# Two band-v transfers at the head of the sync queue joined into one, with the identity matrix behind it

## Chip, cores and metric

The kernel runs on one core of one Trainium2 chip. The metric is device microseconds (us) of one execution; the time before is 297.66 us, the median of three runs (297.59 to 299.77).

## What is computed

The reference is a sparse attention layer followed by a feed-forward block. q, k and v have the shape (8, 8, 576, 64): batch, heads, positions, head size. Heads 0 to 3 use a local band mask (a position sees itself and the 31 before it), heads 4 to 7 a strided causal mask (positions that are equal modulo 32).

```
scores = q @ k^T / 8, masked with -1e9       # per batch and head
attn   = softmax(scores)
x      = (attn @ v), heads side by side      # (4608, 512)
h      = x @ w_in                            # (512, 2048)
g      = s * relu(h)**2 + b
out    = g @ w_out                           # (2048, 512), float32
```

## The kernel before

The work is emitted by a planner (`Plan`, `lay_out`): every matmul group is a step with a cost and with needs, and a small model of the five engines decides in which order the steps of attention, of the first feed-forward product (`ff1`) and of the second (`ff2`) are written. The order is fixed when the kernel is built. On the chip each engine walks its own list in order and waits on semaphores.

A batch element has four pairs of heads: m = 0 and 1 are the band pairs (names with `_loc`, tiles of 96 queries, `LQ`), m = 2 and 3 the strided ones (`_str`, tiles of 72). For the first batch element q and k arrive with positions on partitions and are transposed on TensorE by a matmul against an identity matrix, the tile `ident` (L527 for the band pairs). The results go to PSUM and are copied by ScalarE or VectorE to `qD_loc` and `kT_loc` (L437). Then the scores of a tile are two matmuls into one bank: L653 adds the mask, as `ident` times `negs`, and L656 adds k times q. ScalarE takes the exponential (L674), L717 multiplies by v, VectorE normalises (L734, L744), and `x_nat` is transposed back (L764).

There are two ways for data to come in. GpSimd (POOL) issues the transfers that change fp32 to fp16, one after the other in its own list: `ql` and `kl` of the first pair, `ql` and `kl` of the second (L378), `qs` and `ks` (L405), v of the second band pair (L1399), `vs` (L405). SyncE (SP) issues plain copies. At its head stood, in this order: `ident` (L346, 128 rows of 256 bytes), v of head 0 and v of head 1 in the band layout (L344, each 96 partitions by 6 runs of 64 fp32 numbers, so 576 runs of 256 bytes), and `negs` (L348, 128 rows of 672 bytes). Behind them SP waits for `ql` of the second pair (L1396), and only then issues `masks` and the two scalars.

The two heads of v land as fp32 in `vl_stage`, which is a view of the later home of `w_out` (so the trace calls it `w_out_sb`), and POOL casts them to `v_loc` (L437, one cast for each head, then a copy of the 32 rows that lie before a tile). Only after that, and after a small copy that waits for `qs` (L1420), does POOL issue the four transfers of `w_in` (L427).

While PE waits in the first 14 us, the planner writes filler matmuls into its list (`keep_running`, L1536), which multiply a tile of ones into a bank that nobody reads. Their number and place are fixed when the kernel is built.

Of the kernel before, what the change touches and what calls it, by code (L numbers as in the profile page):

```python
# [204 lines left out]
@with_exitstack  # L205
def kernel(
    ctx: ExitStack,
    tc: tile.TileContext,
    q: bass.AP,
    k: bass.AP,  # L210
    v: bass.AP,
    moe_w_in: bass.AP,
    moe_w_out: bass.AP,
    moe_s: bass.AP,
    moe_b: bass.AP,
    out: bass.AP,
):
    shapes = q.shape, out.shape, moe_w_in.shape
    lay_out(ctx, tc, tc.nc, q, k, v, moe_w_in, moe_w_out, moe_s, moe_b, out, ORDER, *shapes)


def lay_out(ctx, tc, nc, q, k, v, moe_w_in, moe_w_out, moe_s, moe_b, out, order, q_shape, out_shape,
# [14 lines left out]
    LQ, LT, LPAD = 96, 6, 32  # L237
# [64 lines left out]
    def x_free(b):  # L302
# [23 lines left out]
    vl_stage = w_out_sb.rearrange("p f m -> p (f m)").bitcast(FP32)[:, 0:NL // 2].rearrange(  # L326
        "p (h t d) -> p h t d", h=2, d=D)
# [7 lines left out]
    def v_band(b, h):  # L335

        return v[b, h].rearrange("(t p) d -> p t d", p=LQ)
# [1 line left out]
    def h4(ap):  # L339
        return ap.rearrange("p (h x) -> p h x", h=4)  # L340

    def stage_v(heads):
        for h in heads:
            nc.sync.dma_start(out=vl_stage[LPAD:128, h], in_=v_band(0, h))  # L344

    nc.sync.dma_start(out=ident, in_=h_ident.ap())  # L346
    stage_v(range(2))
    nc.sync.dma_start(out=negs, in_=h_neg.ap())  # L348
    nc.vector.memset(ones16, 1.0)
    for i in range(2):  # L350
# [1001 lines left out]
    def fetch_qk(b):  # L1352
        for mm in range(2):
            if (b - 1, "kTs", mm) in loaded:

                nc.gpsimd.tensor_copy(out=gate[0:1, 2 + mm:3 + mm],  # L1356
                                      in_=loaded[b - 1, "kTs", mm][0:1, 0, 0:1])
        load_qk(b)
        for name in ("q", "k"):
            if b >= (QB_DMA if name == "q" else KB_DMA):  # L1360
                arrive(both(name + "l", b), landing(4600))
                continue
            if b < HEAD_T:
                arrive(both(name + "l", b), landing(2400 if name == "q" else 2600))
                continue
            plan.done["raw", name, b] = landing(1700 if b > 1 else 2400 if name == "q" else 2500)
            for mm in range(2):
                pair_post(b, name, mm, ("raw", name, b))
        for name in ("qs", "ks"):
            arrive(both(name, b), landing(2000 if b > 1 else 1200))  # L1370
# [23 lines left out]
    def after_landing(i, src):  # L1394
# [5 lines left out]
        out=v_loc[0].rearrange("p h t d -> p (h t) d")[LPAD:128, 2 * LT:4 * LT, 0:D],  # L1400
        in_=v.rearrange("b h (t p) d -> b p (h t) d", p=LQ)[0, :, 2 * LT:4 * LT])
# [58 lines left out]
    for b in range(B):  # L1460
        for m in range(4):
            steps, last_av = pair_steps(b, m)
            att.append(steps)
            if b + 2 < B:

                if m == 0:
# [5 lines left out]
                        lambda eng, b=b: fetch_qk(b + 2), [("fetch", b + 2)])  # L1472
# [157 lines left out]
```

## Time and profile before

| what | value |
|---|---|
| median of three runs | 297.66 us (297.59 to 299.77) |
| profiled execution, its own time | 298.37 us |
| span of the profiled execution | 296.5 us |
| PE busy | 289.6 us, 98% of the span |
| PEld, DVE, ACT, POOL busy | 74%, 80%, 66%, 31% |
| DMA, software queue (issued by POOL) | 60848 packets, 18.23 MB |
| DMA, hardware queue (issued by SP) | 45270 packets, 19.51 MB |
| granted TensorE clock, mean | 1.00 |

The span runs from the first to the last instruction that the profiler records; the time of the same execution is 1.9 us longer than its span. "Busy" is time in which an engine has an instruction running; a line such as L527 is a line of the kernel before; an arrow `out<-in` gives the tile written and the tiles read. Rows of DMA issues on SP carry the name SPq. In a view of one queue the columns are packets, megabytes, and the time of the packets as a share of sixteen DMA engines over the stretch asked for.

### The profile page before, as it was taken

How to read it: one execution, taken by the hardware profiler on the slowest of the kernel's cores; microseconds unless marked ns; L12 is line 12 of the kernel's file. 1: busy time of each engine (PE TensorE's matmuls, PEld its weight loads, DVE VectorE, ACT ScalarE, POOL GpSimd, SP SyncE). 2: the span in 40 equal slices, each digit the busy share in tenths (PEclk: the TensorE clock that was granted, in tenths of full speed). 3: DMA queues.
4: the chain of work that ended last, by engine and by line, in shares of the span. 5: the costliest groups of instructions: out<-in, count | busy, mean ns of one | idle time of the engine just before them, and what ended most of it. 6: DMA issues, size and time to landing. Idle time of an engine off the chain costs nothing.

```text
span 296.5 us, 7100 instructions
## 1 busy us (share of the span) xinstructions
PE 289.6 (98%) x2800; PEld 218.9 (74%) x2800; DVE 236.3 (80%) x498; ACT 194.4 (66%) x334; POOL 92.2 (31%) x140
## 2 busy tenths in 40 slices
PE   7999999999999999999999999999999999999995
PEld 3775665665565567889767885778888999999984
DVE  5865977888976789768886888688799689888873
ACT  3677855897967797948873777477966564576500
POOL 8772623700970395007920087200001000000000
PEclk9999999999999999999999999999999999999999
DMA  8999999999999899959999999998230300210314
GB/s 131 190 207 203 205 177 179 202 189 130 136 155 156 100 90 170 164 109 132 175 145 137 165 168 149 146 127 211 47 93 20 108 35 2 71 38 2 107 39 143
DMA packets 106152, 38.19 MB, mean 129 GB/s; under 512 B 85414, under 2 KB 103974, under 8 KB 106118
## 3 DMA queue, kind: packets, MB, share of 16 engines
q0 software_dynamic: 60848, 18.23, 65.4%
q1 hardware_dynamic: 45270, 19.51, 36.6%
q8 instruction: 22, 0.36, 0.6%
q14 instruction: 12, 0.10, 0.1%
HBM read 36.99 MB, written 10.62 MB: 161 GB/s over the span
## 4 chain that ended last, share of the span: by engine, by line
PE 78%; DMA 15%; POOL 4%; issue 1%; DVE 1%; ACT 0%; SPq 0%; POOLq 0%; DVEq 0%
PE ps_f L1016 28%; PE ps_f L984 22%; PE ps_f L1271 6%; DMA v_loc<-in_v_dram 5%; DMA ks<-in_k_dram 5%; PE ps_s L656 4%; PE ps_f L1241 3%; DMA kT<-ks 3%; DMA vs<-in_v_dram 2%; PE ps_a L717 2%; PE ps_t L1241 2%; PE ps_a L1241 2%; PE ps_s L1241 2%; PE ps_s L984 2%; PE ps_t L984 1%; PE ps_s L1271 1%
## 5 line engine op out<-in xcount | busy, mean ns | idle before, releaser
L1016 PE MATMUL ps_f<-xT,w_in_sb 128*128 128x512 f16 (+4 forms) x568 | 115.3, 331 | 0.0
L1042 ACT ACTIVATE u<-ps_f 128x512 f16<-128x512 f32 x107 | 62.8, 594 | 34.5 <-PE ps_f L1016 32.4
L1016 PEld LDWEIGHTS <-w_in_sb 128*128 128x128 f16 x576 | 57.1, 114 | 23.1
L984 PEld LDWEIGHTS <-gT 128*128 128x128 f16 x608 | 58.3, 98 | 8.6
L984 PE MATMUL ps_f<-w_out_sb,gT 128*128 128x256 f16 x376 | 53.4, 273 | 0.0
L1271 PE MATMUL ps_f<-w_out_sb,gT 128*128 128x512 f16 x112 | 31.9, 379 | 0.0
L674 ACT ACTIVATE p_str<-ps_s 72x432 f16<-72x432 f32 (+1 forms) x45 | 21.1, 487 | 10.4 <-PE ps_s L656 9.8
L1052 DVE TENSOR_TENSOR gT<-u 128x1024 f16<-128x1024 f16 x32 | 21.8, 682 | 5.2 <-ACT u L1042 4.8
L1050 ACT ACTIVATE gT<-u 128x1024 f16<-128x1024 f16 x24 | 25.4, 1058 | 0.7
L984 PE MATMUL ps_f<-w_mix,gT 128*128 128x256 f16 x176 | 24.9, 273 | 0.0
L674 ACT ACTIVATE p_loc<-ps_s 128x384 f16<-128x384 f32 x46 | 20.7, 489 | 5.9 <-PE ps_s L656 5.4
L744 DVE TENSOR_TENSOR x_nat<-ps_a,rec 72x384 f16<-72x384 f32 (+2 forms) x45 | 23.5, 523 | 0.7
L852 DVE TENSOR_TENSOR gT<-gT 128x1024 f16<-128x1024 f16 x34 | 22.4, 683 | 0.3 <-ACT gT L1050 0.3
L415 POOL DMA_DIRECT2D v_loc<-in_v_dram x24 | 17.8, 762 | 9.6 <-DVE x_nat L744 3.7
L984 PEld LDWEIGHTS <-S 128*128 128x128 f16 x176 | 17.1, 98 | 2.8
L717 PEld LDWEIGHTS <-p_str 72*128 72x128 f16 x256 | 13.6, 98 | 5.7 <-ACT p_str L674 0.7
L1271 PEld LDWEIGHTS <-gT 128*128 128x128 f16 x128 | 11.4, 98 | 6.9 <-issue 0.2
L420 POOL DMA_DIRECT2D v_str<-in_v_dram x16 | 13.0, 816 | 11.0 <-PE ps_f L1016 3.5
L1356 POOL COPY gate<-kT 1x1 f16<-1x1 f16 x6 | 1.6, 266 | 47.1 <-DMA kT<-ks 47.1
L734 DVE RECIPROCAL rec<-ps_a 72x6 f32<-72x6 f32 (+2 forms) x45 | 8.3, 184 | 9.0 <-PE ps_a L717 8.8
L717 PEld LDWEIGHTS <-p_loc 128*128 128x128 f16 x192 | 11.2, 98 | 5.3 <-ACT kTs L437 0.8
L984 PE MATMUL ps_f<-w_mix,S 128*128 128x256 f16 x112 | 15.0, 273 | 0.0
(233 smaller groups left out, 542.2 us busy)
## 6 DMA issues: line engine op xcount, KB each, us to landing
out_dram<-o SPq DMA_DIRECT2D x34, 256.0 KB
w_in_sb<-in_moe_w_in_dram POOLq DMA_DIRECT2D x4, 512.0 KB, 10.4
w_out_sb<-in_moe_w_out_dram POOLq DMA_DIRECT2D x4, 512.0 KB, 9.8
qs<-in_q_dram POOLq DMA_DIRECT2D x6, 288.0 KB, 7.6
ks<-in_k_dram POOLq DMA_DIRECT2D x6, 288.0 KB, 9.4
v_loc<-in_v_dram POOLq DMA_DIRECT2D x24, 72.0 KB, 10.5
ql<-in_q_dram POOLq DMA_DIRECT2D x4, 288.0 KB, 9.7
kl<-in_k_dram POOLq DMA_DIRECT2D x16, 72.0 KB, 4.1
```

The source lines that it names most:

```text
L415: nc.gpsimd.dma_start(out=vl[LPAD:128, h, :, 0:D], in_=v_band(b, h))
L674: nc.scalar.activation(out=st["pw", g][0:nk, 0:2 * n * nq], in_=st["s", g][0:nk, 0:2 * n * nq], func=AF.Exp, scale=scale)
L717: nc.tensor.matmul(out=st["pa", g][:, n % 6, :], lhsT=st["pw", gp_][0:nk, i * nq:i * nq + WIDE], rhs=vt[0:nk, 2 * mm + e, j, :])
L744: nc.vector.tensor_tensor(out=x_at(0, cnt), in0=st["pa", g][0:nq, 0:cnt, 0:D], in1=st["rec", g][0:nq, 0:cnt].to_broadcast([nq, cnt, D]), o ...
L852: {"V": nc.vector, "P": nc.gpsimd}[eng].tensor_tensor(out=at(out), in0=at(x), in1=at(y), op=op)
L984: nc.tensor.matmul(out=gts[name, T, t][:, 0] if halves else gts[name, T][:, t], lhsT=lhs(k, t), rhs=rhs(k), start=fresh and k == 0 and (ha ...
L1016: nc.tensor.matmul(out=gts["h", T, ft][:, lo:hi], lhsT=w_in_sb[ft // 4][:, ct].rearrange("p (x l) -> p l x", l=4)[:, ft % 4], rhs=xT[ct][: ...
L1042: nc.scalar.activation(out=u, in_=gts["h", T, ft], func=AF.Relu)
L1050: nc.scalar.activation(out=g, in_=u, func=AF.Square)
L1052: nc.vector.tensor_tensor(out=g, in0=u, in1=u, op=ALU.mult)
L1241: nc.tensor.matmul(out=st[bk][:, 256 * t:256 * t + 256], lhsT=lhs(t, c), rhs=rhs(c), start=fresh and t == c == 0, stop=t == c == 1, skip_g ...
L1271: nc.tensor.matmul(out=gts[id_], lhsT=gts[T][:, ft, ts * 128:(ts + 1) * 128], rhs=w_out_sb[:, ft, cols], start=(ft == 0), stop=(ft == NFT ...
```

## The change

The helper `stage_v` and its call are removed. In its place one transfer brings both heads of v: partition p takes 12 runs of 64 numbers (2 heads by 6 tiles) instead of 6 in each of two transfers. It stands first in the list of SP, `ident` second, `negs` third. Source, destination, and the bytes of every run are the same.

```diff
-    def stage_v(heads):
-        for h in heads:
-            nc.sync.dma_start(out=vl_stage[LPAD:128, h], in_=v_band(0, h))
-
+    nc.sync.dma_start(
+        out=vl_stage[LPAD:128].rearrange("p h t d -> p (h t) d"),
+        in_=v.rearrange("b h (t p) d -> b p (h t) d", p=LQ)[0, :, 0:2 * LT])
     nc.sync.dma_start(out=ident, in_=h_ident.ap())
-    stage_v(range(2))
     nc.sync.dma_start(out=negs, in_=h_neg.ap())
```

The lists of PE, DVE, ACT and POOL keep their instructions and their order; SP's has one transfer fewer. The first transpose of PE (L527) waits for `ident` as before, now the second transfer of SP; both casts of POOL now depend on the one transfer of v, where each depended on its own. The lines of the changed kernel are numbered two lower from there on.

## The prediction

> **What bounds the kernel now.** I read the page first (busy shares), then who waited for whom on PE, then the rows of the first 10 us in order of time, then the DMA queues over short stretches of those microseconds.
>
> ```profile
> PE 289.6 (98%) x2800; PEld 218.9 (74%) x2800; DVE 236.3 (80%) x498; ACT 194.4 (66%) x334; POOL 92.2 (31%) x140
> ```
>
> PE is busy for 289.6 of 296.5 us, and the stretches 60 to 120, 120 to 180 and 240 to 290 us show it busy all the time. So a microsecond lost at the start moves the end by a microsecond, unless an early wait of PE takes it up. The waits of PE, longest first:
>
> ```profile
> PE ps_t L527 <- DMA ql<-in_q_dram: 1.1, 1, 1.1
> PE ps_s L1536 <- DVE w_mix L349: 1.1, 1, 1.1
> PE ps_f L717 <- DVE v_loc L437: 0.7, 1, 0.7
> ```
>
> The first is the place of the change: the first transpose needs `ql` and `ident`, and `ql` came last. The rows around it (start, duration, engine; behind x the count, in brackets the idle time before):
>
> ```profile
> 0.74 0.35 SPq L346 DMA_DIRECT2D ident<-ident  x1
> 1.16 0.99 SPq L344 DMA_DIRECT2D w_out_sb<-in_v_dram  x2
> 2.19 0.52 SPq L348 DMA_DIRECT2D w_mix<-negs  x1
> ...
> 1.06 3.68 PE L1536 MATMUL ps_s<-w_mix 128*128 128x512 f16 x10 [1.06 <-DVE w_mix L349]
> 5.84 0.45 PE L527 MATMUL ps_t<-ident,ql 96*64 96x96 f16 x12 [1.10 <-DMA ql<-in_q_dram]
> 6.22 0.94 PE L1536 MATMUL ps_s<-w_mix 128*128 128x256 f16 x6
> 7.09 0.45 PE L527 MATMUL ps_a<-ident,kl 96*64 96x96 f16 x12
> 7.46 0.77 PE L1536 MATMUL ps_s<-w_mix 128*128 128x512 f16 x3
> 8.16 0.45 PE L527 MATMUL ps_f<-ident,ql 96*64 96x96 f16 x12
> ...
> 7.25 1.23 POOL L405 DMA_DIRECT2D vs<-in_v_dram  x2
> 8.48 0.96 POOL L437 CAST v_loc<-w_out_sb 128x384 f16<-128x384 f32 x2
> ```
>
> Read here: SP has issued everything by 2.7 us, PE stands still from 4.74 to 5.84, and POOL goes from its last issue into the casts of v without a gap, so v is not late today. Last, what the queue of SP (q1) moved: in the stretches 2.1 to 3.25, 3.25 to 4.3 and 4.3 to 5.3 us (packets, MB, share of 16 engines):
>
> ```profile
> q1 hardware_dynamic: 592, 0.15, 55.8%
> ...
> q0 software_dynamic: 131, 0.10, 76.5%
> q1 hardware_dynamic: 108, 0.03, 18.7%
> ...
> q1 hardware_dynamic: 572, 0.18, 81.1%
> q0 software_dynamic: 92, 0.06, 39.0%
> ```
>
> Alone, q1 moves 592 packets in 1.15 us (515 per us). While POOL's queue q0 is full it moves 108 in 1.05 us, about as many as q0 (131). When q0 pauses, it moves 572 per us.
>
> **The change, part by part.**
>
> *One issue less on SP.* The two issues of v take 0.99 us together, one alone 0.44 to 0.50. The new one, with as many runs as both, takes between 0.44 and 0.99 us. `ident` is then issued between 1.2 and 1.8 us, `negs` up to 0.6 us sooner or not at all sooner. Behind them SP waits for `ql` of the second pair until 7.66, which does not move. Worth nothing: SP's own list is hidden by that wait of 4.9 us. Nobody else is queued behind it.
>
> *The identity goes behind v.* This is the only step that can cost. Before `ident` was issued at 0.74, and up to 2.1 us q1 had moved 144 packets, its 128 rows and 16 completion writes: 3 us and more ahead of `ql`. Now it stands behind 96 x 12 = 1152 packets of v and their 16 completions. With its own 144 the queue has to move 1312 packets before PE may start. I work out when by the three paces above:
>
> - Packets begin about 1.0 us after an issue starts (`ident`: 0.74 to 1.68; first v: 1.16 to 2.24, by the first slices of the queue that are not empty). So v begins at 1.75.
> - 1.75 to 3.25 at 515 per us: 772.
> - 3.25 to 4.3, q0 full: 108, together 880.
> - The other 432 at 572 per us: 0.76 us. The last packet of `ident` moves at 5.06.
> - From the last packet to the waiting engine: the packet records put the last packet of the first `ql` at 5.24, and PE started at 5.84, so 0.6. PE could see `ident` at 5.66, 0.18 us before `ql`.
>
> So the identity is no longer early; it arrives nearly together with `ql`. Bounds: below, the slow stretch doesn't hit q1 (515 per us throughout): 1312/515 = 2.55 us, last packet at 4.3, seen by PE at 4.9, 0.94 us before `ql`. Just above the middle, the DMA engine that is last: the second v transfer of today has its last rows at 5.6 (27 of its packets fall between 5.3 and 5.9), and at that moment an engine has moved just what it must move for v and `ident` together. PE would then start at 6.2, late by 0.36. Far above, q1 stays at the pace of the slow stretch: (1312 - 772)/103 per us = 5.2 us, last packet at 8.5, PE starts at 9.1, late by 3.2 us. I take late by 0.2 us, between the middle estimate (early by 0.18) and the engine that comes last (0.36), since those two rows are of the same packets on the same queue; the far end would need a q0 that never pauses, while today's pauses because POOL needs 0.6 us to issue each transfer.
>
> *Who takes up a late start.* Behind the first transposes PE runs six fillers, then the transposes of `kl`, before which its weight loads stood idle 0.16 us for `kl`; then three fillers, and the transposes of the second `ql`, with 0.37 us of idle before. Together 0.53 us that are there to be filled. On ScalarE the copy of q (6.33 to 7.61) is followed by 1.70 us of idle; on DVE the copy of `kT_loc` waited 1.65 us and ends at 8.34, before the scores at 8.86. So a start that is late by 0.2 us costs 0; by 0.36 us, 0; by 3.2 us, 3.2 - 0.53 = 2.7 us. The cover is gone beyond 0.53 us, and from there each microsecond of lateness is one of the result; next late would be the exponential at 9.31 and then v's product at 10.07.
>
> [...]
>
> *One transfer for both heads, and the casts.* The first cast waited for one head, now for both. 1168 packets by the same paces: 880 at 4.3, the rest in 0.5 us, 4.8 plus 0.6 is 5.4 us, against 8.48 when POOL comes to the cast. Far bound: 288/103 = 2.8, 7.1 plus 0.6 is 7.7, still before 8.48. Cost 0, hidden by POOL's issues (1.28 to 8.48); if that cover were gone, the casts, L1420 and the four loads of `w_in` would be late in turn. `negs` follows `ident` with 144 packets: 5.3 plus 0.6 against its use at 8.78, 0 as well.
>
> *What can be won.* Nothing but the waits of PE ahead of 8.2 us, and these hang on q0. In the slow stretch q1 used 18.7% of the engines' time, over 1.05 us 0.2 us; from 5.3 to 5.9 us 14.7%, 0.1 us. If v were through before, `ql` and `kl` could land up to 0.3 us sooner. Between 0 and -0.3 I take 0, as the same packets of v still fall into the slow stretch.
>
> Sum: 0 (SP) + 0 (late identity, covered) + 0 (casts) + 0 = 0, on 298.37 us of the profiled execution with its span of 296.5; the median is 0.71 lower, and to it the change is applied: 297.66, say 297.7.
>
> **Rivals.**
> (1) *The identity is late and its lateness is paid.* For: 1312 packets in one queue that slows to a fifth when q0 is full. Against: the 572 packets per us of 4.3 to 5.3. Decides from a last packet later than 5.24 + 0.53 = 5.77 us. With half of the far bound, 1.6 us late, 1.1 us cost: 298.8; all of it, 300.4.
> (2) *The clock of PE falls back in the longer gap*, the one on the other side. The first ten fillers start 0.42 us apart, against 0.86 us for four of the same width later (0.216 each): PE began at half pace and got the full one about 2.9 us after its first matmul. The gap of 1.1 us did not bring it back. If `ident` comes at the far bound, the gap is 4.74 to 9.1, 4.3 us; should the clock fall in it, the next 2.9 us run at half pace, 1.45 us more: 2.7 + 1.45 = 4.2, 301.8 us, slower by 1.4%. It decides at a gap length that no row here shows, over 1.1 us. [...]
> (3) *A gain*: q0 gets more turns, `ql` and `kl` land 0.3 us sooner: 297.4. For: no break between the two v transfers. Against: POOL's issue times set most of it.
> (4) *Nothing at all moves*, as every part is hidden: 297.7; it can be told from the forecast by the wait before L527 only.
>
> **How the numbers follow.** The forecast (identity about when `ql` comes, covered; with rival 4) 0.66; rival 1 0.14, a fifth of it near its end; rival 2 0.06; rival 3 0.09; anything in the long stretch that answers to other arrival times, 0.05, of either sign. A measurement of this kernel can tell about 1% (2.98 us) from no change. Over 1% faster (below 294.7): 0.03, from the last case alone. Over 1% slower (above 300.6): 0.06 from rival 2, 0.02 from the end of rival 1, 0.02 from the last, 0.10. Within: 0.87. The range runs from 297.0 (rival 3, and 0.4 for the spread between runs) to 299.8 (most of rival 1); beyond it lie rival 2, the end of rival 1 and the last case.
>
> **What would show it.** Right: SP's rows begin with one issue of v of 0.4 to 1.0 us; L527 starts between 5.8 and 6.3 us, its wait given to `ident` or `ql`; the idle before the second `ql` shrinks from 0.37; the casts begin at 8.5; granted clock 1.00; PE busy all through 60 to 180. Rival 1: L527 after 6.4 us and every later row shifted alike. Rival 2: matmuls 0.42 us apart behind the gap. The forecast is wrong if the span moves by over 1.5 us with L527 in its place.

## The result and the profile after

The changed kernel takes 299.33 us in the median of 22 runs, the kernel before 297.57 us in as many of its own; disturbed runs left out, the ratio is 1.0055 (95% interval 1.0035 to 1.0075). So it is slower by 0.55%: inside the range, inside "within 1%", and not the zero of the forecast. The spread says more than the median: 20 of the 22 runs of the changed kernel lie above 298 us, 2 of the 22 of before; the fastest are close (297.40 and 297.05).

The profiled execution has a span of 297.8 us (its own time 299.54), 1.3 us more than before. The page's first row, then the waits of PE:

```profile
PE 291.6 (98%) x2800; PEld 219.7 (74%) x2800; DVE 236.3 (79%) x498; ACT 194.5 (65%) x334; POOL 93.1 (31%) x140
```

```profile
PE ps_s L1534 <- DVE w_mix L347: 1.1, 1, 1.1
PE ps_f L715 <- DVE v_loc L435: 1.0, 1, 1.0
PE ps_t L525 <- DMA ql<-in_q_dram: 0.7, 1, 0.7
```

The wait before the first transposes (L525 now) is shorter, 0.7 for 1.1 us, and still put down to `ql`, not to the identity. But PE is busy 2.1 us longer with the same 2800 matmuls (291.65 against 289.55 in the view by stretches), and idle 0.8 us less: 1.3 us. Matmuls that take longer, not a longer wait, are the difference. The rows in order of time show where:

```profile
0.74 0.40 SPq L342 DMA_DIRECT2D w_out_sb<-in_v_dram  x1
1.20 0.59 SPq L345 DMA_DIRECT2D ident<-ident  x1
1.83 0.43 SPq L346 DMA_DIRECT2D w_mix<-negs  x1
8.49 0.74 SPq L1394 DMA_DIRECT2D gate<-ql  x1
...
1.06 4.34 PE L1534 MATMUL ps_s<-w_mix 128*128 128x512 f16 x10 [1.06 <-DVE w_mix L347]
6.07 0.69 PE L525 MATMUL ps_t<-ident,ql 96*64 96x96 f16 x12 [0.68 <-DMA ql<-in_q_dram]
6.70 1.68 PE L1534 MATMUL ps_s<-w_mix 128*128 128x256 f16 x6
8.30 0.69 PE L525 MATMUL ps_a<-ident,kl 96*64 96x96 f16 x12
8.93 1.35 PE L1534 MATMUL ps_s<-w_mix 128*128 128x512 f16 x3
10.21 0.46 PE L525 MATMUL ps_f<-ident,ql 96*64 96x96 f16 x12
...
8.75 0.56 POOL L403 DMA_DIRECT2D vs<-in_v_dram  x1 [0.62 <-DMA ql<-in_q_dram]
9.31 1.75 POOL L435 CAST v_loc<-w_out_sb 128x384 f16<-128x384 f32 x3
```

The ten fillers take 4.34 us for 3.68, the six 1.68 for 0.94, the three 1.35 for 0.77: half pace, up to about 10 us. In the clock records full pace begins at 10.27 us, before at 3.93. (The column of granted clock says 1.00 ahead of the first recorded switch, so in these microseconds the pace is read from the rows.) The second `ql` transposes come at 10.21 for 8.16, 2.05 us late. That the span is only 1.3 us longer is in part the other profile's doing: the profiled execution of the kernel before, with 298.37 us one of its longer ones, stands still at two later places, 0.22 us at 48.6 us and 0.21 us at 204.1 us. Against experiments 1 and 7 below, with spans of 295.3 us, the changed kernel's profile is 2.5 us longer. Two smaller things: `ql` is seen at 6.07 for 5.84, and SP's own wait for the second `ql` ends at 8.49 for 7.66; POOL waited for the same transfer between its two issues of `vs` and came to the casts at 9.31 for 8.48. The queues in the stretches 2.1 to 3.25, 3.25 to 4.3 and 4.3 to 5.3 us:

```profile
q1 hardware_dynamic: 1125, 0.28, 108.0%
q0 software_dynamic: 8, 0.01, 12.0%
...
q0 software_dynamic: 82, 0.06, 55.7%
q1 hardware_dynamic: 60, 0.03, 26.9%
...
q0 software_dynamic: 175, 0.13, 85.5%
q1 hardware_dynamic: 107, 0.06, 35.9%
```

The joined v runs without a break: 1125 packets in 1.15 us where it was 592. By the packet records the last run of 256 bytes, which v and the identity consist of, moves at 3.44 us (3.32 and 3.66 in two more profiles of this kernel): the identity is 2 us early, not late. POOL's queue pays: 82 packets for 131 in the next stretch, though q1 moves only 60 there.

### The profile page after: what moved, and what is told of

Same layout as the page of the kernel before. It is cut to its first block, busy times and chain, and to the rows that moved or that the text cites. A ratio compares the mean times of both kernels' runs of the same rounds, so it can differ in the third digit from the quotient of the medians.

```text
span 297.8 us, 7099 instructions
## 1 busy us (share of the span) xinstructions
PE 291.6 (98%) x2800; PEld 219.7 (74%) x2800; DVE 236.3 (79%) x498; ACT 194.5 (65%) x334; POOL 93.1 (31%) x140
## 4 chain that ended last, share of the span: by engine, by line
PE 96%; DMA 2%; DVE 1%; issue 0%; ACT 0%; POOLq 0%
PE ps_f L1014 32%; PE ps_f L982 25%; PE ps_f L1269 8%; PE ps_s L654 5%; PE ps_f L1239 3%; PE ps_a L715 3%; PE ps_t L1239 2%; PE ps_s L982 2%; PE ps_s L1239 2%; PE ps_a L1239 2%; DMA ql<-in_q_dram 2%; PE ps_t L715 1%; PE ps_t L982 1%; PE ps_s L1269 1%; PE ps_s L1534 1%; PE ps_f L715 1%
```

## The experiments

Two theories stood at the start. **C**: a longer gap before the first transposes keeps PE at half pace for some microseconds more. **D**: only landing times count, whatever the pace. A third, **I**: the identity itself is late. Each experiment is compared with the kernel before on the same chip; the first four kernels shared one chip, the next four a second, the last four a third.

### 1. Joined, identity first

```diff
+    nc.sync.dma_start(out=ident, in_=h_ident.ap())
     nc.sync.dma_start(out=vl_stage[LPAD:128]..., in_=v...[0, :, 0:2 * LT])
-    nc.sync.dma_start(out=ident, in_=h_ident.ap())
     nc.sync.dma_start(out=negs, in_=h_neg.ap())
```

> The joined transfer of v stays, the identity goes back to the head of SP's list. Theory C (pace of PE): the gap of PE before its first transposes got longer (0.68 us at half pace, against 0.5 us if the before kernel ran at half pace), so that PE comes to full pace some microseconds later in many executions. What lengthens the gap is the first ql, seen by PE 0.23 us later because one joined burst of v (1125 packets from 2.1 to 3.25 us) and the negs behind it meet POOL's first transfers; so the identity's place is of no matter and the median stays at 299 to 299.7. Theory D (landing times alone): same cause, no pace; also 299 to 299.7, with ql seen after 6.0 us. Theory I (identity late): 297.6.

Measured 297.35 us (12 runs, 297.09 to 298.27), ratio 0.9989 (0.9971 to 1.0007). Joining alone did not cost there, against C and D as I had put them; theory I had 297.6. Its rows:

```profile
1.05 4.34 PE L1534 MATMUL ps_s<-w_mix 128*128 128x512 f16 x10 [1.05 <-DVE w_mix L347]
5.65 0.59 PE L525 MATMUL ps_t<-ident,ql 96*64 96x96 f16 x12 [0.26 <-DMA ql<-in_q_dram]
6.18 0.94 PE L1534 MATMUL ps_s<-w_mix 128*128 128x256 f16 x6
```

The ten fillers run at half pace here too (4.34 us). But `ql` is seen at 5.65, the gap is 0.26 us for 0.68, and full pace comes at 6.01: the six fillers behind it take 0.94 us.

### 2. Order alone

```diff
-    nc.sync.dma_start(out=ident, in_=h_ident.ap())
     stage_v(range(2))
+    nc.sync.dma_start(out=ident, in_=h_ident.ap())
     nc.sync.dma_start(out=negs, in_=h_neg.ap())
```

> v stays in two transfers, only the identity goes behind them. Theory I (identity late): the identity lands at about 5.6 to 6.2 us and the median is 299 or more, with the wait of the first transposes put down to the identity. Theories C and D (joined burst): the break between the two v transfers stays, ql lands as before, and the median is 297.6, unless the identity itself is seen after 6.0 us, when C expects a part of the loss (298 to 299).

Measured 298.26 us (297.07 to 299.92), ratio 1.0020 (1.0002 to 1.0038). This is the one kernel whose wait names the identity:

```profile
PE ps_f L527 <- DMA ql<-in_q_dram: 0.7, 1, 0.7
PE ps_t L527 <- DMA ident<-ident: 0.7, 1, 0.7
```

Its last run of 256 bytes moves at 4.81 us, PE starts at 5.36. So behind two transfers the identity is what PE waits for, at a time that still does no harm (before: 5.84). Theory I fits the name on the wait and not the loss: it had 299 or more, C and D 297.6, and the small loss lies between. In this profile PE also waits 0.7 us for the second `ql`, POOL comes to its casts at 9.28 us, and PE waits 0.5 us for them.

### 3. The changed kernel with two more fillers

```diff
+    for _ in range(2):
+        nc.tensor.matmul(
+            out=ps["s0"], lhsT=ones16, rhs=ones16[:, None, :].to_broadcast([128, 4, 128]),
+            start=True, stop=True)
     while i2 < len(f2) or any(at_i[p] < len(att[p]) for p in range(len(att))):
```

> The changed kernel with two more filler matmuls of 512 columns ahead of the ten, so that PE hardly stands still before its first transposes. Theory C: PE comes to full pace in its second or third stretch whatever the phase, median back to 297.4 to 298.3 and a narrow spread; the fillers start 0.42 us apart only to about 5 or 6 us. Theory D: ql lands as late as before this edit, median 299.2 or higher, since fillers change no transfer.

Measured 298.02 us (297.25 to 298.80), ratio 1.0017 (1.0002 to 1.0032). No transfer was touched, PE got 0.4 to 0.85 us more to do, and the times over 299 us are gone (13 of 22 in the changed kernel, measured apart from these, 0 of 12 here). C foresaw this, D did not. Full pace at 6.76.

### 4. The kernel before with two fillers less

```diff
+    skipped = [0]
...
     def keep_running(until):
...
+        if skipped[0] < 2:
+            skipped[0] += 1
+            plan.emit(Step(lambda: None, 128 * n / ghz + 3))
+            return True
         plan.emit(Step(f, 128 * n / ghz + 3))
```

> The kernel before without two of its ten first fillers, all transfers as they were. The gap of PE before the first transposes is 0.85 us longer (1.3 to 2 us). Theory C: PE comes to full pace later in many executions, median 298.5 to 300 and a wider spread. Theory D: nothing waits for fillers, 297.6.

Measured 299.32 us (6 runs, 298.56 to 303.44), ratio 1.0058 (1.0038 to 1.0077): the loss of the changed kernel, made from the kernel before by taking work away.

```profile
1.05 3.49 PE L1538 MATMUL ps_s<-w_mix 128*128 128x512 f16 x8 [1.05 <-DVE w_mix L349]
5.59 0.69 PE L527 MATMUL ps_t<-ident,ql 96*64 96x96 f16 x12 [1.04 <-DMA ql<-in_q_dram]
6.21 1.67 PE L1538 MATMUL ps_s<-w_mix 128*128 128x256 f16 x6
```

`ql` comes early here (5.59), and SP sees the second `ql` only 0.15 us later than in the kernel before (7.81 for 7.66); still the six fillers take 1.67 us, and full pace begins at 9.71. The gap of 1.04 us behind half pace was enough in this profile. D, by which landing times alone count, can't explain the loss; C can.

### 5 and 6. The changed kernel twice more

> The changed kernel once more, beside its rivals on one chip. Theory C2 (gap and pace): the first ql is seen after 5.85 us more often than with the identity first, and where the gap before the first transposes is over about 0.6 us with PE still at half pace, the full pace comes only at 9 to 10.5 us. Median 298.5 to 299.5, wide spread. The view of waits names ql, not the identity, since all of q1's runs of 256 bytes are through by 3.5 us. Theory I (the identity itself is late): the wait is put down to the identity, and the first transposes start over 6.2 us.

> The changed kernel a third time, for one more profile. C2: if the first ten fillers end at 4.6 to 5.0 us (pace came early), span 295.3 to 296.8 us; if they end at 5.4 us, the start of the first transposes decides: before 5.8 us a span below 297, after 5.9 us full pace only at 9 us or later and a span of 297 to 299. Theory D (landing alone): the span follows the start of the first transposes, whatever the pace.

Measured 299.47 us (12 runs, 297.46 to 301.98), ratio 1.0042 (1.0013 to 1.0072), and 300.96 us for the single run. Both profiles have `ql` far later than I expected, 7.36 and 7.07 us. Rows of the first, and its view by stretches (busy times of PE, PEld, DVE, ACT and POOL, then the granted clock, the DMA share and GB/s):

```profile
1.05 3.92 PE L1534 MATMUL ps_s<-w_mix 128*128 128x512 f16 x10 [1.05 <-DVE w_mix L347]
7.36 0.45 PE L525 MATMUL ps_t<-ident,ql 96*64 96x96 f16 x12 [2.38 <-DMA ql<-in_q_dram]
7.74 1.63 PE L1534 MATMUL ps_s<-w_mix 128*128 128x256 f16 x6
...
7.89 0.90 POOL L1397 DMA_DIRECT2D v_loc<-in_v_dram  x1 [1.47 <-DMA ql<-in_q_dram]
```

```profile
4.50:7.80 3.30, 0.92 (x16) 0.41 (x15) 1.16 (x14) 0.00 (x0) 1.92 (x4) 1.00 1.22 177
7.90:11.20 3.30, 3.30 (x21) 1.32 (x20) 0.76 (x1) 1.21 (x2) 3.24 (x6) 0.50 1.40 190
11.30:14.70 3.40, 3.37 (x65) 2.79 (x66) 2.54 (x6) 1.54 (x4) 3.34 (x6) 1.00 1.38 154
```

Here full pace came early (4.41), PE then stood for 2.38 us, and the clock went back to 0.50 from 7.82 to 11.24. The third profile has the same: full at 5.03, half at 8.44, full at 11.86, behind a gap of 1.79 us. The switches are 3.41 or 3.42 us apart in both, by these times. Why the same kernel takes 297.4 us in one execution and 301 in another, and whether that hangs on when these steps begin, no run here shows.

So there are two ways into the loss, both through a late `ql`: pace that did not come (first profile), and pace that was lost again (the other two). That I had tied C to half pace alone was too narrow, and the expectation for the third run, which knew only that way, missed it: its fillers ended at 5.28.

### 7. Identity first, a second time

> Joined transfer with the identity first, a second time, beside the changed kernel on one chip. If the place of the identity is what costs, 297.1 to 297.7 again with a narrow spread; if the first measurement was the luck of a chip, it comes as wide as the changed kernel, 298.5 or more. C2 expects ql seen between 5.5 and 5.8 us.

Measured 298.19 us (12 runs, 297.11 to 300.06), ratio 1.0030 (1.0007 to 1.0052), on the chip on which the changed kernel took 299.47. Neither expectation: not as narrow as the first time, not as wide as the changed kernel. Its profiled execution is one of the good ones (gap 0.86 us at full pace, span 295.3). The first result was partly luck. The medians differ by 1.3 us on this chip and, across chips, by 2.0, but on this chip the intervals of the two ratios overlap (1.0013 to 1.0072 for the changed kernel): what the place of the identity is worth is not shown by the times.

### 8. Identity first with a quarter filler more

```diff
+    nc.tensor.matmul(
+        out=ps["s0"][:, 0:256], lhsT=ones16, rhs=ones16[:, None, :].to_broadcast([128, 2, 128]),
+        start=True, stop=True)
     while i2 < len(f2) or any(at_i[p] < len(att[p]) for p in range(len(att))):
```

(on the kernel of experiment 1)

> Joined transfer with the identity first and one filler of 256 columns more at PE's head, 0.21 us at half pace, so that the fillers end at 5.6 us where PE has not come to full pace. C2: the few slow executions go, median 297.0 to 297.5 and nothing above 298. Theory D: no difference to the identity first, 297.4.

Measured 297.64 us (297.19 to 298.53), ratio 1.0005 (0.9989 to 1.0020). Against experiment 7 on the same chip: 0.55 us off the median, and none of 12 runs over 299 us for 4 of 12. The direction is that of C, but the intervals of 7 and 8 overlap, and four runs stayed over 298, where I had expected none.

### 9 to 12. What makes ql late

Three edits of the changed kernel, and one of the kernel before:

```diff
 # 9: a 4-byte transfer ahead of v
+    nc.sync.dma_start(out=sb_row[0:1, 0:1], in_=moe_s[None, :])
     nc.sync.dma_start(out=vl_stage[LPAD:128]..., in_=v...[0, :, 0:2 * LT])
...
-    nc.sync.dma_start(out=sb_row[0:1, 0:1], in_=moe_s[None, :])
 # 10: no transfer of negs
-    nc.sync.dma_start(out=negs, in_=h_neg.ap())
...
     nc.vector.memset(part32, 1.0 / 32)
+    nc.vector.memset(negs, 0.0)
 # 11: one filler of 512 columns more in the kernel before
+    nc.tensor.matmul(out=ps["s0"], lhsT=ones16, rhs=..., start=True, stop=True)
 # 12: the identity on another queue
-    nc.sync.dma_start(out=ident, in_=h_ident.ap())
+    nc.scalar.dma_start(out=ident, in_=h_ident.ap())
```

> The changed kernel with the transfer of the scalar s (4 bytes) moved from its later place to the head of SP, so that the joined v is issued some 0.35 us later, as it is where the identity stands first; the identity stays behind v. Theory B (when the burst starts): a burst of v that starts at 0.74 us ends just when POOL's first ql begins (3.0 us) and its first reads take about 1 us; with the burst later, ql is seen by 5.8 us and the median is 297.2 to 298.2. Theory P (the identity's place behind v itself): no difference to the changed kernel, 299 to 299.7.

> The changed kernel without the transfer of negs; the mask of the first batch element is left out, VectorE writes zeros in its place after its other memsets. Theory N (negs): the 128 runs of 672 bytes that follow the burst from 3.4 us on are what slows ql; without them ql is seen by 5.8 us, median 297.2 to 298.2. Theory B and P: ql stays late, 299 or more.

> The kernel before with one more filler of 512 columns at PE's head (0.43 us at half pace, 0.22 at full). Theory C (gap and pace): the few executions of the kernel before between 298 and 300 go, median 297.1 to 297.5, at most 0.1% from before. Without C: no difference at all in the spread, or up to 0.4 us slower.

> The changed kernel with the identity issued by ScalarE at its head, on a queue of its own; v is first on SP, then negs. Theory B: v still starts at 0.74 us, ql late, 299 or more. Theory P: the identity no longer stands behind v, 297.2 to 298.2.

Measured on one chip: 9, 298.44 us, ratio 1.0021 (0.9997 to 1.0045). 10, 298.16 us, 1.0023 (1.0002 to 1.0045). 11, 297.28 us, 0.9995 (0.9977 to 1.0013). 12, 299.24 us, 1.0031 (1.0002 to 1.0061).

12 speaks against the identity's place itself: taken out of v's queue, it leaves the median at 299.24, and the wait of 1.3 us still names `ql`, though the interval does not exclude the 297.2 to 298.2 of theory P:

```profile
1.06 4.34 PE L1534 MATMUL ps_s<-w_mix 128*128 128x512 f16 x10 [1.06 <-DVE w_mix L347]
6.69 0.45 PE L525 MATMUL ps_t<-ident,ql 96*64 96x96 f16 x12 [1.29 <-DMA ql<-in_q_dram]
7.07 0.94 PE L1534 MATMUL ps_s<-w_mix 128*128 128x256 f16 x6
9.01 0.45 PE L525 MATMUL ps_f<-ident,ql 96*64 96x96 f16 x12
...
PE ps_s L654 <- DMA kT<-ks: 1.1, 1, 1.1
```

Two things stand in this profile that a median hides. Full pace came at 6.10 us, inside the gap: the fillers behind it take 0.94 us, and the start costs just what `ql` is late, 0.85 us at the first and at the second transposes. And the last row is a wait of another kind, for a transposed `ks` at 205 us. Compared matmul by matmul with experiment 1, this profile is 0.8 us late behind the start and loses 1.7 us more around 205 us. The same wait is 0.9 us in experiment 10, 0.6 in experiment 3 and in the third profile of the changed kernel, 0.4 in experiment 2, 0.2 in experiment 8 and the kernel before, and not in the list for the other two profiles of the changed kernel and experiments 1, 4, 7, 9 and 11. So the times of 2, 3, 10 and 12 are not a measure of the start alone, while those two profiles of the changed kernel and experiment 4 lose nearly all at the start (2.2, 3.0 and 1.4 us, counted in the same way). What sets this wait, no run shows.

9 and 10 lie a microsecond lower, but their intervals overlap that of 12, so neither the start of the burst nor `negs` is shown to be the cause alone. Experiment 9 came out between its two theories, and its profile still has `ql` at 6.26. Experiment 10 came out as theory N had it, with `ql` by 5.49 and 298.16 us, but `ql` landed as soon once with `negs` too (experiment 3). The DMA view's row for the two transfers of `ql` (median us from issue to landing) orders the profiles:

| kernel | `ql`, us to landing |
|---|---|
| before; experiments 4 and 11, same transfers | 4.7; 4.6, 4.5 |
| identity first, joined: experiments 1, 7, 8 | 4.3, 4.4, 4.4 |
| order alone: experiment 2 | 4.8 |
| changed kernel, three profiles; experiment 3, same transfers | 5.2, 6.2, 5.7; 4.4 |
| experiments 9, 12 | 5.0, 5.3 |
| experiment 10 (no `negs`) | 4.6 |

With v joined at the head (at most 4 bytes ahead of it) and `negs` kept, `ql` took 5.0 to 6.2 us in five of six profiles; experiment 3 is the sixth, with 4.4. With the 32 KB of the identity ahead of v it took 4.3 to 4.7 in all six. That the burst at the head slows POOL's first transfers is thus seen in most profiles; by what, is not settled. In the packet records the slowest single packet of `ql` or `kl` that starts before 6 us takes 0.92, 1.59 and 0.85 us in the three profiles of the changed kernel, and 0.30 to 0.86 where the identity is ahead: the ranges touch.

In 11 no execution is over 299 us (0 of 12, against 3 of 35 before), which 12 runs of the kernel before would often show as well, and two stayed over 298. Its interval covers 1: no version here beats the kernel before by what can be measured.

## Why the prediction was right and wrong

**Right: SP, the wait for v. By luck: the range.** The one issue takes 0.40 us (foreseen 0.44 to 0.99) and SP's own wait hides it. v was never waited for. The loss stayed within 1%, and the interval of the ratio, 1 to 2.2 us, lies where rival 1 had put half its far bound (1.1 us). That is luck: the range reached up to 299.8 for a late identity, and the identity was early. The forecast of no change failed at two terms of the sum: a late start that was to be covered, and a pace of PE that was to stay as it was.

**Wrong: the three paces of q1.** I carried 515, 103 and 572 packets per us over from the two transfers, and had the last identity packet at 5.06 us. It moved at 3.44: the joined transfer ran at 978 per us and was through ahead of the slow stretch, which had met the second of two transfers only. I had read 131 against 108 packets there as what a full q0 leaves to q1. Packets of q0 beside it do not alone make it slow: in experiment 1 the joined v was still in its queue, and in the same 3.25 to 4.3 us q1 moved 319 packets beside 161 of q0, on the chip on which the two transfers of experiment 4 moved 128 beside 139. In the kernel before the slow stretch begins just where the first v transfer is through (704 runs of 256 bytes by 3.25 us, 128 of the identity and 576 of v). Why the next transfer is held up there, no run shows; in experiment 9, where the identity is issued at 1.55 us for 1.20, the last such run moves at 5.46. Where the transfers are not joined (experiment 2) the identity was indeed last, seen at 5.36 for my 5.66. Nor do I see a gain in turns for q0 (rival 3) in the changed kernel: q0 moved 82 packets there for 131 before, though q1 moved only 60, and how two queues share an engine no run shows.

**Wrong: the term that wasn't in the sum.** Under "what can be won" I priced what q0 gains when v is out of the way, 0 to -0.3 us, and never what it loses while a denser burst runs. Identity first shows the gain (`ql` lands in 4.3 us for 4.7). The changed kernel shows the loss: seen 0.23, 1.23 and 1.52 us later than in the profile of before.

**Wrong: the cover.** The 0.16 and 0.37 us are idle times of the weight loads (PEld), which run beside the matmuls: from 6 to 7 us 0.62 us of loads in a microsecond in which PE was busy throughout. PE itself had none to fill; the profile of before says so in its rows and in its view by stretches, in which the first pair behind the length is PE:

```profile
7.08 0.31 PEld L527 LDWEIGHTS <-kl 96*64 96x64 f16 x12 [0.16 <-DMA kl<-in_k_dram]
8.16 0.31 PEld L527 LDWEIGHTS <-ql 96*64 96x64 f16 x12 [0.37 <-issue]
...
6.00:7.00 1.00, 1.00 (x18) 0.62 (x14) 0.00 (x0) 0.66 (x2) 1.00 (x2) 1.00 1.24 183
7.00:8.00 1.00, 1.00 (x17) 0.52 (x15) 0.42 (x1) 0.61 (x1) 0.97 (x3) 1.00 1.26 194
8.00:9.00 1.00, 1.00 (x21) 0.77 (x20) 0.68 (x2) 0.00 (x0) 1.00 (x3) 1.00 1.25 198
```

So at full pace a late start is paid in full: in experiments 9 and 12 the first transposes come 0.42 and 0.85 us later than in the kernel before, and the second `ql` transposes (8.58 and 9.01 for 8.16) just as much later. At half pace the fillers between take 1.68 for 0.94 and 1.35 for 0.77 us, and 0.23 us of lateness became 2.05.

**Right mechanism, wrong trigger: rival 2.** I gave the clock 0.06, an estimate, and asked for a gap of over 1.1 us that only the far bound would bring. One of the two ways was missed: a gap ahead of full pace. Behind gaps of 0.68 us (changed kernel) and 1.04 (experiment 4) full pace came only at 10.27 and 9.71 us, for 3.93 before. The other way was as described: behind gaps of 1.79 and 2.38 us it was gone again, both shorter than the 4.3 us of the far bound. The price, 301.8 us, is about that of the longest runs; the loss in the median, 1.8 us, is less than half of it, and some executions escape it (the fastest took 297.40 us).

**Missed: POOL's own issues.** I had POOL at its casts at 8.48 for certain. It waits for earlier transfers between its issues, and with `ql` late it came at 9.31 in the first profile. In that one the casts ended (11.06) before their use at 12.12. In experiment 2, with full pace and the casts from 9.28, PE waited 0.5 us for them.

**What stays open.** Why `ql` slows behind the joined burst, and what PE must do to come to full pace. I count steps of 3.41 us back from the first recorded switch, an estimate, as no record ahead of it shows that they hold there. Then the changed kernel has a gap of 0.68 us and twelve small transposes between 3.45 and 6.86 us and was still at half pace behind them, while experiment 12, with 0.70 us of idle and no transposes from 2.69 to 6.10, and experiment 1, with 0.26 us of idle in the 3.41 us up to 6.01, came to full pace at the end. By that count the length of the gap alone does not decide; whether the transposes play a part, no run separates. Also open is the wait at 205 us, perhaps a case of the long stretch answering to other arrival times, for which the prediction kept 0.05.

## What to carry to other kernels

A transfer that is joined and moved up is not only a change of who waits for it: here it landed as a burst (1125 packets for 592 in 1.15 us), and the first transfer of another queue paid for it in most profiles (`ql` landed in 5.2 to 6.2 us for 4.7). At the start of a kernel look at the pace of PE together with its idle time: fillers that end just ahead of the first real work were a margin here (with two more of them the ratio was 1.0017 for 1.0055), and a gap of 0.68 us for 0.26 went with full pace at 10.27 us for 6.01. Weight loads that stood idle for 0.16 and 0.37 us were no slack of PE, which was busy all through 6 to 9 us: ask the view by stretches whether PE itself was busy. When the median moves by half a percent and the spread grows by more, compare the distributions and several profiles; one profile shows one execution.

## Not expected of the hardware

Full pace came to stay at 3.72 to 11.86 us in these profiles of nearly the same start; where it came and went, the switches were 3.41 or 3.42 us apart. Two transfers of 576 runs of 256 bytes moved 592 packets in 1.15 us, one of 1152 runs 1125 in the same time; a part of the difference is the earlier start, as the two transfers moved 958 where they stood first (experiment 2). From the last packet of `ql` to the waiting matmul it took 0.6 us (5.47 to 6.07).
